# Late attention in strided-query order, with a new start for blocks 0 and 1: one change to a chunked-attention and gated feed-forward kernel

## The chip, the cores and the metric

The kernel runs on one core of a Trainium2 chip. The metric is device time in microseconds (us) of one execution. Each time below is a median of several executions; the profile shows one execution, and its span is about 2 us shorter than the time (260.4 and 262.46 us in the kernel before). The engines are named as the profile names them: PE (TensorE matmul), PEld (TensorE weight load), DVE (VectorE), ACT (ScalarE), POOL (GpSimd), SP (SyncE, here only the issuer of transfers).

## The reference

Chunked attention with a few memory rows, followed by a gated feed-forward network. Cut to what matters:

```python
# q, k, v: [4 batches, 8 heads, 768 rows, 64]; mem_k, mem_v: 8 rows per head
for c in range(24):                       # chunks of 32 queries
    l, r = max(0, 32*c - 16), min(768, 32*c + 40)
    k_full = concat(mem_k, k[:, :, l:r]); v_full = concat(mem_v, v[:, :, l:r])
    out[:, :, 32*c:32*c+32] = softmax(q_c @ k_full.T / 8) @ v_full
x = out as [3072 tokens, 512]
y = (relu(x @ w_gate) * (x @ w_val)) @ w_out       # 512 -> 1536 -> 512
```

The 3072 tokens are worked on as eight blocks of 384. A block has four attention steps of 96 queries; the keys of a step are a band of 120 rows and 8 memory rows. A block then has 12 feed-forward units (128 of the 1536 columns each: four gate matmuls, relu, four value matmuls, product) and three output products.

## The kernel before

Rows of q, k and v are loaded three to a partition, so that position 3i+t lies in partition i, slot t. After the transpose the queries are therefore in the order "t outer, i inner" (mod-3 order). The kernel before put them back into natural order when the exponential was written, which makes that write hop by three elements. These are the parts that matter (cuts marked):

```python
def diag(n):                              # block-diagonal queries, two DVE copies a block
    for x in range(2):
        dv(qd_t[n % 2][D * x:D * x + D, :, x, :], qT_t[n % 2][D * x:D * x + D].rearrange("p a t c -> p a (t c)"))
class Step:
    def scores(self):                     # ... early blocks 0, 1: two 64-row matmuls per head pair, from qp
        pe.matmul(o[...], lhsT=self.kb[:, a, j, :], rhs=qd_t[i][:, a]...)   # late: one 128-row matmul per pair
    def soft(self):                       # late:
        act.activation(e.rearrange("p h (c t) -> p h t c", t=R3),           # writes every third element
                       s_ps.rearrange("p h (t c) -> p h t c", t=R3), ACT.Exp, scale=SCALE)
    def mask(self):   dve.tensor_tensor(out=e, in0=e, in1=m8, op=ALU.mult)
    def values(self): ...                 # 8 matmuls with the masked exponentials as weights
    def norm(self):   ...                 # DVE: divide by the row sums
def dff(n, m):                            # one feed-forward unit
    ... gate matmuls; act Relu -> g_relu; value matmuls
    dve.tensor_tensor(out=gvT[n][:, m, c0:c1], in0=vl_ps, in1=g_relu[:, 0:w], op=ALU.mult)
# steady loop, block n beside the attention of block n+1
for u in range(NDC + NT):                 # 12 units, then 3 output products
    # u = 4, 6, 8, 10: scores and exp of step j, dff(u), mask; u = 6, 8, 10, 12: values and norm of step j
    ...
    if u == 0: diag(n + 1)
    if u == 1: bands(n + 1, pl)           # key bands, on POOL
```

In these traces ACT and DVE take their instructions in program order. So a long instruction there delays what stands behind it, whether that needs it or not: in the step shown below, the gate matmuls of a relu end at 125.00 us, but relu starts at 125.67, behind an exponential of 1.48 us that it does not read.

The softmax here doesn't subtract the row's maximum and nothing guards it: scores larger than these inputs give would overflow.

Of the kernel before, what the change touches and what calls it, by code (L numbers as in the profile page):

```python
# [15 lines left out]
def kernel(  # L16
# [49 lines left out]
    NG = [3]  # L66
# [18 lines left out]
    vx = wpool.tile([2 * NMEM, H, D], F32, name="vx")  # L85
    kx16 = wpool.tile([2 * NMEM, H, D], F16, name="kx16")
    vx16 = wpool.tile([2 * NMEM, H, D], F16, name="vx16")
    kT_t = [wpool.tile([128, R3 + 1, HP, 128], F16, name=f"kT{i}") for i in range(2)]
    qT_t = [wpool.tile([128, HP, R3, 128], F16, name=f"qT{i}") for i in range(2)]
    qd_t = [wpool.tile([128, HP, 2, MB], F16, name=f"qd{i}") for i in range(2)]  # L90
    kb_t = [wpool.tile([128, HP, NJ, 128], F16, name=f"kb{i}") for i in range(2)]
    vb_t = [wpool.tile([128, NJ, H, VW], F16, name=f"vb{i}") for i in range(2)]
    ex_t = [wpool.tile([128, H, 128], F16, name=f"ex{i}") for i in range(2)]
    id16 = wpool.tile([128, 128], F16, name="id16")
    step3 = wpool.tile([128, DW], F16, name="step3")
    selx = wpool.tile([2 * NMEM, 256], F16, name="selx")
# [12 lines left out]

    def build_mask(name, qb):  # L110
        m = wpool.tile([128, QB], F16, name=name)
        pool.memset(m, 1.0)
        for g in range(QB // 32):
            c = 3 * qb + g
            lo = max(32 * c - 16, 0) - starts[qb]
            hi = min(32 * c + 40, S) - starts[qb]
            sl = m[:, 32 * g:32 * g + 32]
            if lo > 0:
                pool.affine_select(out=sl, in_=sl, pattern=[[0, 32]], compare_op=ALU.is_ge,
                                   fill=0.0, base=-lo, channel_multiplier=1)  # L120
            if hi < BAND:
                pool.affine_select(out=sl, in_=sl, pattern=[[0, 32]], compare_op=ALU.is_ge,
                                   fill=0.0, base=hi - 1, channel_multiplier=-1)
        pool.affine_select(out=m, in_=m, pattern=[[0, QB]], compare_op=ALU.is_ge,
                           fill=1.0, base=BAND - 1, channel_multiplier=-1)
        return m

    masks = {}
# [57 lines left out]
    def diag(n):  # L186
        for x in range(2):
            dv(qd_t[n % 2][D * x:D * x + D, :, x, :], qT_t[n % 2][D * x:D * x + D].rearrange("p a t c -> p a (t c)"))  # L188

    def bands(n, eng, part=(0, 1)):  # L190
        i = n % 2
        kT, kb = kT_t[i], kb_t[i]

        def src(t, off, dims):
            return bass.AP(tensor=t.tensor, offset=t.offset + off, ap=[t.ap[0], [128, HP]] + dims)
# [6 lines left out]
        if 0 in part:  # L202
# [4 lines left out]
            else:  # L207
                e = kT_t[0]
                eng(dst(0, 16, [[R3, 35], [1, R3]]), src(kT, 0, [[1, 35], [TS, R3]]))
                eng(dst(0, 0, [[1, 1]]), src(e, 2 * TS + 122, [[1, 1]]))  # L210
                eng(dst(0, 1, [[R3, 5], [1, R3]]), src(e, 123, [[1, 5], [TS, R3]]))
                eng(dst(3, 0, [[R3, 40], [1, R3]]), src(kT, 88, [[1, 40], [TS, R3]]))
        if 1 in part:
            if i == 0:
                eng(dst(3, 112, [[1, NMEM]]), src(kT, R3 * TS, [[1, NMEM]]))
            eng(dst(0, BAND, [[128, NJ], [1, NMEM]]), src(kT_t[0], R3 * TS + NMEM, [[0, NJ], [1, NMEM]]))
# [5 lines left out]
    class Step:  # L222
        def __init__(self, n, j):
            self.n, self.j, self.kb, self.vb = n, j, kb_t[n % 2], vb_t[n % 2]
            self.early = n in EARLY
            self.mk = masks[kind(NJ * (n % 2) + j)]

        def scores(self):
            i, j = self.n % 2, self.j
            for a in range(HP):  # L230
                if self.early:
                    for x in range(2):
                        pe.matmul(PS[:, x, QB * a:QB * a + QB], lhsT=self.kb[D * x:D * x + D, a, j, :],
                                  rhs=qp[D * x:D * x + D, i, a, QB * j:QB * j + QB], start=True, stop=True)
                else:
                    o = PS[:, a // 2, 256 * (a % 2):256 * (a % 2) + 256].rearrange("p (x c) -> p x c", x=2)
                    pe.matmul(o[:, :, 0:QB].rearrange("p x (t c) -> p x t c", t=R3), lhsT=self.kb[:, a, j, :],  # L237
                              rhs=qd_t[i][:, a].rearrange("p x (t c) -> p x t c", t=R3)[:, :, :, PP * j:PP * j + PP],
                              start=True, stop=True)

        def soft(self):
            self.ex = ex_t[n_exp[0] % len(ex_t)]
            n_exp[0] += 1
            e = self.ex[:, :, 0:QB]
            if self.early:
                act.activation(e.rearrange("p (h b) c -> p b h c", b=2),  # L246
                               PS[:, 0:2, 0:384].rearrange("p b (h c) -> p b h c", h=4), ACT.Exp, scale=SCALE)
            else:
                s_ps = PS[:, 0:2].rearrange("p b (h c) -> p (b h) c", h=4)[:, :, 0:QB]
                act.activation(e.rearrange("p h (c t) -> p h t c", t=R3),  # L250
                               s_ps.rearrange("p h (t c) -> p h t c", t=R3), ACT.Exp, scale=SCALE)

        def mask(self):
            e = self.ex[:, :, 0:QB]
            m = self.mk
# [30 lines left out]
    def dff(n, m, c0=0, c1=MB):  # L286
# [13 lines left out]
        dve.tensor_tensor(out=gvT[n][:, m, c0:c1], in0=vl_ps, in1=g_relu[:, 0:w], op=ALU.mult)  # L300
# [5 lines left out]
    def outp(n, t, last=False):  # L306
# [5 lines left out]
        r0 = n * MB + 128 * t  # L312
        if last:
            act.copy(o_sb[:, 0:256], PS[:, o, 0:256])
            dv(o_sb[:, 256:512], PS[:, o, 256:512])
            sp.dma_start(out[r0:r0 + 128, 0:256], o_sb[:, 0:256])
            act.dma_start(out[r0:r0 + 128, 256:512], o_sb[:, 256:512])
        else:
            act.copy(o_sb, PS[:, o])  # L319
            sp.dma_start(out[r0:r0 + 128, :], o_sb)  # L320
# [3 lines left out]
    def turn3(c, n, a0):  # L324
        o = PS[:, bank(), 0:R3 * 128].bitcast(F16).rearrange("p (a t i) -> p a t i", a=2, t=R3)
        for a in range(2):
            for t in range(R3):
                w = kn[:, n % 2, t, a0 + a, :] if c == "k" else qn[:, n % 2, a0 + a, t, :]
                pe.transpose(o[:, a, t], w, id16)
        return o  # L330

    def turn_k3(n, a0):
        dv(kT_t[n % 2][:, 0:R3, a0:a0 + 2].rearrange("p t a c -> p a t c"), turn3("k", n, a0))

    def turn_q3(n, a0):
        act.copy(qp[:, n % 2, a0:a0 + 2].rearrange("p a (i t) -> p a i t", t=R3),
                 turn3("q", n, a0).rearrange("p a t i -> p a i t"))
# [4 lines left out]
    def gather_v(n, j, eng=None):  # L342
# [3 lines left out]
        sel = selx[:, 128:256] if (i, j) == (0, NJ - 1) else selx[:, 0:128]  # L346
        pe.matmul(o, lhsT=sel, rhs=vx16, start=True, stop=True)
        mm = [(s0 - MB * i - t, i, t) for t in range(R3)]
        if i == 1 and j == 0:
            mm += [(s0 - t, 0, t) for t in range(R3)]  # L350
        for e, (c, w, t) in enumerate(mm):
            pe.matmul(o[0:BAND], lhsT=step3[:, c:c + BAND], rhs=v16[:, w, :, t, :], start=False,  # L352
                      stop=(e == len(mm) - 1), skip_group_check=True)
        (eng or act.copy)(vb_t[i][:, j, :, 0:D], o)
# [3 lines left out]
    for c in "kq":  # L358
        load3(sp, c, 0, 0, 4)
        load3(sp, c, 0, 4, 4)  # L360
    load_kx(sp, 0)
    load3(sp, "v", 0, 0, 4)
    load3(sp, "v", 0, 4, 4)
    sp.dma_start(vx[NMEM:2 * NMEM], mem_v[0].rearrange("h n d -> n h d"))
    sp.dma_start(vx[0:NMEM], rows(v, 0, MB, NMEM))
    load3(sp, "k", 1)
    load3(sp, "q", 1)
    load3(sp, "v", 1)

# [4 lines left out]
    def keep(n):  # L374
        for _ in range(n):
            pe.matmul(PS[:, 7], lhsT=zero[:, 0:128], rhs=zero, start=True, stop=True)  # L376
# [6 lines left out]
    dve.memset(kT_t[0][:, R3, 0, 0:2], 0.0)  # L383
    act.activation(warm, warm, ACT.Exp)
    steps(id16, 0, -1)
    steps(step3, -DPAD, -R3)
    for c in (0, 128):
        steps(selx[:, c:c + 128], -(BAND - NMEM), -1)
    pool.memset(selx[0:NMEM, 0:128], 0.0)
# [4 lines left out]
    for m, qb in (("first", 0), ("int", 1)):  # L394
        masks[m] = build_mask(f"mask_{m}", qb)
# [16 lines left out]
    keep(9)  # L412
    cast3(dv, "k", 0, 0, 2)
    turn_k3(0, 0)
    cast3(dv, "k", 0, 2, 2)
    keep(2)
    turn_k3(0, 2)
    bands(0, dv, (0,))
    cast3(pl, "q", 0, 0, 2)
    act.copy(kx16, kx[:, 0])  # L420
    keep(1)
    turn_q3(0, 0)
    cast3(pl, "q", 0, 2, 2)
    keep(2)
    turn_q3(0, 2)
    o = PS[:, 3, 0:HP * NMEM].bitcast(F16).rearrange("p (a c) -> p a c", a=HP)
    for a in range(HP):
        pe.transpose(o[:, a], kx16[:, 2 * a:2 * a + 2, :].rearrange("n x d -> n (x d)"), id16[0:2 * NMEM, 0:2 * NMEM])
    act.copy(kT_t[0][:, R3, :, 0:2 * NMEM], o)
    bands(0, dv, (1,))  # L430
    keep(3)
    cast_v3(act.copy, 0, 0, 4)
    pl(vx16, vx)
    cast_v3(dv, 0, 4, 4)

    masks["last"] = build_mask("mask_last", NQB - 1)
    st = [Step(0, j) for j in range(NJ)] + [Step(1, j) for j in range(NJ)]

    def pipe(s, mid=(), end=()):
        if s < 2 * NJ:  # L440
            st[s].scores()
            st[s].soft()
            st[s].mask()
        for f in mid:
            f()
        if s < 2 * NJ:
            gather_v(s // NJ, s % NJ)
        if 1 <= s <= 2 * NJ:
            st[s - 1].values()
            st[s - 1].norm()  # L450
        for f in end:
            f()
        if s >= 2:
            st[s - 2].turn_pe(act.copy if s % 2 else dv)

    pipe(0, [lambda: keep(3)])
# [4 lines left out]
    pipe(1)  # L461
    cast3(pl, "q", 1, 0, 2)
    cast3(pl, "q", 1, 2, 2)
    pipe(2, (), [lambda: turn_k3(1, 0)])
    load_w(256, 256)
    pipe(3, (), [lambda: turn_k3(1, 2), lambda: turn_q3(1, 0)])
    cast_v3(pl, 1, 0, 4)
    cast_v3(pl, 1, 4, 4)
    turn_q3(1, 2)
    bands(1, dv)  # L470
    load_w(512, 512)
    load_w(1024, 512)
    for c in (0, 4, 8):
        load_wo(c)
    pipe(4)
    NG[0] = 4
    pipe(5)
    pipe(6, (), [lambda: dff(0, 0)])
    pipe(7, (), [lambda: dff(0, 1)])
    pipe(8, (), [lambda: dff(0, 2)])  # L480
# [149 lines left out]
```

## Time and profile before

| | before |
|---|---|
| time, median of 3 | 262.46 us |
| profiled span | 260.4 us |
| start: until block 1's first unit | 40.25 us |
| middle: from there until block 2's first unit | 47.75 us |
| five blocks with attention beside them (2 to 6) | 144.64 us |
| last block and end | 27.7 us |

The stages are read from the timeline: each boundary is the start of the first gate matmul of that unit. From the page, the busy time of the engines and the granted clock in the 40 slices of the span (tenths of full speed):

```profile
PE 235.4 (90%) x1611; PEld 131.5 (50%) x1611; DVE 124.1 (48%) x257; ACT 128.4 (49%) x197; POOL 49.3 (19%) x96
...
PEclk9998899999999899999999999999999999999999
```

PE is the bound, but 90% busy hides waits, since the records of matmuls overlap: most of those with 384 columns last 326 ns, and the next one starts after 162. A better measure is the distance between starts: 162 ns for 384 columns and 216 ns for 512 when nothing is in the way.

The groups of instructions by form (line, engine, operation, shapes, count, then busy us and mean ns, then the idle time ahead and who ended it):

```profile
L250 ACT ACTIVATE ex<-PS 128x768 f16<-128x768 f32 x24 | 35.2, 1468 | 20.3 <-PE PS L237 20.2
L246 ACT ACTIVATE ex<-PS 128x768 f16<-128x768 f32 x8 | 6.5, 814 | 3.8 <-PE PS L233 3.8
L188 DVE COPY qd<-qT 64x1536 f16<-64x1536 f16 x12 | 8.4, 696 | 4.8 <-DMA qT<-qn 4.8
```

The first two lines do the same arithmetic on the same 768 elements. L250 (late blocks) writes every third element, L246 (blocks 0 and 1) writes runs of 96: 1468 ns against 814.

One step of a steady block in the timeline (start, duration, engine, what, and in brackets the idle time ahead of it; other lines of the stretch are left out):

```profile
123.86 0.49 PE L237 MATMUL PS<-qd,kb 128*128 128x192 f16 x4
124.39 1.48 ACT L250 ACTIVATE ex<-PS 128x768 f16<-128x768 f32 x1 [1.42 <-PE PS L237]
125.67 0.51 ACT L296 ACTIVATE g_relu<-PS 128x384 f16<-128x384 f32 x1
126.14 0.81 PE L298 MATMUL PS<-xT,w_val_sb 128*128 128x384 f16 x4
126.22 0.56 DVE L300 TENSOR_TENSOR gvT<-PS,g_relu 128x384 f16<-128x384 f32 x1 [0.93 <-ACT g_relu L296]
126.69 0.55 DVE L257 TENSOR_TENSOR ex<-ex,mask_first 128x768 f16<-128x768 f16 x1
127.39 0.42 PE L261 MATMUL PS<-vb,ex 128*128 128x66 f16 x8 [0.43 <-DVE ex L257]
```

The exponential ends at 125.87. Relu stands behind it on ACT (its record starts at 125.67, since neighbours on one engine overlap a little in the record), then come the product gv, the mask, and the value matmuls. From the start of the matmul ahead of the values (the last of the four L298, near 126.63) to the values' start the trace has 0.75 us instead of 0.16, so PE loses about 0.59 us, in each of four steps of five blocks.

### The profile page before, as it was taken

The page shows a single profiled execution, that of the slowest core. Times are in us where ns is not written, and L with a number is a line of the kernel's source. Part 1 is how long each engine was busy: PE and PEld are TensorE (multiplying, and loading weights), DVE is VectorE, ACT ScalarE, POOL GpSimd, SP SyncE. Part 2 cuts the span into 40 slices and gives each one's busy share as a digit, 9 for nine tenths or more (in the row PEclk, how much of TensorE's full clock was granted, in tenths as well). Part 3 has the DMA queues.
Part 4 walks back from the last instruction along what each step waited for, and adds up shares of the span by engine and source line. Part 5 has one row for each costly group of instructions (what it writes and reads, how often), then busy time and mean ns, then how long its engine had stood idle before and what let it go on. Part 6 is the DMA issues. An engine that isn't in the chain of part 4 may idle for free.

```text
span 260.4 us, 4350 instructions
## 1 busy us (share of the span) xinstructions
PE 235.4 (90%) x1611; PEld 131.5 (50%) x1611; DVE 124.1 (48%) x257; ACT 128.4 (49%) x197; POOL 49.3 (19%) x96
## 2 busy tenths in 40 slices
PE   8895899999989698898989989898899998999993
PEld 3353565666444355544554555445564555446641
DVE  3776573444654057604673076605753276504410
ACT  2564554365357256643673457443772555333321
POOL 6499920000000500006000420006000500000000
PEclk9998899999999899999999999999999999999999
DMA  6999999849973997159941997179912801121012
GB/s 209 312 270 138 183 207 247 219 94 177 294 193 115 202 285 131 30 124 259 237 96 32 241 281 146 33 168 276 234 39 71 198 0 33 30 86 39 0 40 82
DMA packets 84381, 39.37 MB, mean 151 GB/s; under 512 B 57096, under 2 KB 81416, under 8 KB 84360
## 3 DMA queue, kind: packets, MB, share of 16 engines
q1 hardware_dynamic: 78408, 34.25, 54.2%
q0 software_dynamic: 5808, 4.72, 12.1%
q8 instruction: 12, 0.20, 0.3%
q10 hardware_dynamic: 144, 0.13, 0.1%
q14 instruction: 9, 0.07, 0.1%
HBM read 30.05 MB, written 6.29 MB: 140 GB/s over the span
## 4 chain that ended last, share of the span: by engine, by line
PE 56%; DVE 16%; issue 8%; DMA 7%; ACT 6%; SPq 3%; POOL 0%; ACTq 0%; DVEq 0%; POOLq 0%
PE PS L309 19%; PE PS L298 14%; PE PS L293 13%; DVE gvT L300 5%; DVE ex L257 5%; PE PS L261 4%; ACT g_relu L296 4%; DMA qT<-qn 3%; DVE x_big L270 3%; DMA vraw<-in_mem_v_dram 2%; PE PS L352 2%; DMA vx<-in_v_dram 2%; PE PS L237 2%; SPq L141 2%; DVE qd L188 1%
## 5 line engine op out<-in xcount | busy, mean ns | idle before, releaser
L300 DVE TENSOR_TENSOR gvT<-PS,g_relu 128x384 f16<-128x384 f32 x96 | 53.0, 556 | 96.3 <-PE PS L298 75.0
L293 PE MATMUL PS<-xT,w_gate_sb 128*128 128x384 f16 x384 | 78.7, 328 | 2.7 <-issue 2.2
L298 PE MATMUL PS<-xT,w_val_sb 128*128 128x384 f16 x384 | 79.1, 329 | 2.1 <-DVE gvT L300 1.9
L296 ACT ACTIVATE g_relu<-PS 128x384 f16<-128x384 f32 x96 | 47.8, 498 | 43.4 <-PE PS L293 22.4
L309 PE MATMUL PS<-w_out_sb,gvT 128*128 128x512 f16 x288 | 64.1, 379 | 0.0
L298 PEld LDWEIGHTS <-w_val_sb 128*128 128x128 f16 x384 | 37.8, 99 | 28.1 <-issue 3.8
L293 PEld LDWEIGHTS <-w_gate_sb 128*128 128x128 f16 x384 | 37.2, 98 | 25.9 <-issue 4.3
L250 ACT ACTIVATE ex<-PS 128x768 f16<-128x768 f32 x24 | 35.2, 1468 | 20.3 <-PE PS L237 20.2
L309 PEld LDWEIGHTS <-gvT 128*128 128x128 f16 x288 | 27.7, 98 | 31.4
L319 ACT COPY o_sb<-PS 128x512 f32<-128x512 f32 x23 | 13.5, 587 | 44.9 <-PE PS L309 43.0
L204 POOL COPY kb<-kT 128x320 f16<-128x320 f16 (+1 forms) x15 | 11.0, 830 | 130.2 <-DMA kT<-kn 130.2
L261 PE MATMUL PS<-vb,ex 128*128 128x66 f16 x256 | 13.6, 195 | 9.9 <-DVE ex L257 8.7
L270 DVE TENSOR_TENSOR x_big<-PS,rinv 96x512 f16<-96x512 f32 x32 | 22.0, 686 | 1.1
L261 PEld LDWEIGHTS <-ex 128*128 128x128 f16 x256 | 11.1, 99 | 20.4 <-ACT g_relu L296 15.6
L257 DVE TENSOR_TENSOR ex<-ex,mask_int 128x768 f16<-128x768 f16 x24 | 14.1, 586 | 7.3 <-ACT ex L246 3.9
L237 PE MATMUL PS<-qd,kb 128*128 128x192 f16 x96 | 11.8, 245 | 0.1
L188 DVE COPY qd<-qT 64x1536 f16<-64x1536 f16 x12 | 8.4, 696 | 4.8 <-DMA qT<-qn 4.8
L165 ACT CAST qn<-qraw 128x768 f16<-128x768 f32 x12 | 10.0, 836 | 0.0
L267 DVE RECIPROCAL rinv<-PS 96x8 f32<-96x8 f32 x32 | 6.4, 201 | 7.5 <-PE PS L261 5.4
L165 ACT CAST kn<-kraw 128x768 f16<-128x768 f32 x12 | 9.9, 827 | 0.0
L376 PE MATMUL PS<-zero 128*128 128x512 f16 x20 | 7.7, 519 | 1.3 <-DVE zero L378 1.3
L352 PE MATMUL PS<-v,step 128*120 128x512 f16 x27 | 8.8, 450 | 0.0
(90 smaller groups left out, 122.7 us busy)
## 6 DMA issues: line engine op xcount, KB each, us to landing
out_dram<-o_sb SPq DMA_DIRECT2D x23, 256.0 KB
vraw<-in_v_dram SPq DMA_DIRECT2D x24, 240.0 KB
kraw<-in_k_dram SPq DMA_DIRECT2D x7, 768.0 KB
qraw<-in_q_dram SPq DMA_DIRECT2D x7, 768.0 KB
w_out_sb<-in_moe_w_out_dram POOLq DMA_DIRECT2D x3, 512.0 KB, 18.1
w_gate_sb<-in_moe_w_gate_dram POOLq DMA_DIRECT2D x2, 512.0 KB, 10.4
w_val_sb<-in_moe_w_val_dram POOLq DMA_DIRECT2D x2, 512.0 KB, 12.0
kraw<-in_k_dram SPq DMA_DIRECT2D x2, 384.0 KB
```

Source lines behind the costliest of these rows:

```text
L165: eng(d.rearrange("p a t (x d) -> p a x t d", x=2), raw[c][:, i, 2 * a0:2 * a0 + 2 * na].rearrange("p (a x) t d -> p a x t d", x=2))
L237: pe.matmul(o[:, :, 0:QB].rearrange("p x (t c) -> p x t c", t=R3), lhsT=self.kb[:, a, j, :], rhs=qd_t[i][:, a].rearrange("p x (t c) -> p x ...
L250: act.activation(e.rearrange("p h (c t) -> p h t c", t=R3), s_ps.rearrange("p h (t c) -> p h t c", t=R3), ACT.Exp, scale=SCALE)
L257: dve.tensor_tensor(out=e, in0=e, in1=m8, op=ALU.mult)
L261: pe.matmul(PS[:, 2 + h // 4, VW * (h % 4):VW * (h % 4) + VW], lhsT=self.ex[:, h, :], rhs=self.vb[:, self.j, h, :], start=True, stop=True)
L270: dve.tensor_tensor(out=self.x.rearrange("p (b h d) -> p b h d", b=2, h=4), in0=o[:, :, :, 0:D], in1=rb, op=ALU.mult)
L293: pe.matmul(g_ps, lhsT=w_gate_sb[:, f, 128 * m:128 * m + 128], rhs=xTs[n][:, f, c0:c1], start=(f == 0), stop=(f == NFC - 1))
L296: act.activation(g_relu[:, 0:w], g_ps, ACT.Relu)
L298: pe.matmul(vl_ps, lhsT=w_val_sb[:, f, 128 * m:128 * m + 128], rhs=xTs[n][:, f, c0:c1], start=(f == 0), stop=(f == NFC - 1))
L300: dve.tensor_tensor(out=gvT[n][:, m, c0:c1], in0=vl_ps, in1=g_relu[:, 0:w], op=ALU.mult)
L309: pe.matmul(PS[:, o], lhsT=gvT[n][:, m, 128 * t:128 * t + 128], rhs=w_out_sb[:, m, :], start=(m == 0), stop=(m == NDC - 1))
L352: pe.matmul(o[0:BAND], lhsT=step3[:, c:c + BAND], rhs=v16[:, w, :, t, :], start=False, stop=(e == len(mm) - 1), skip_group_check=True)
```

## The change

It has several parts.

1. The late exponential writes contiguous rows. Queries stay in mod-3 order through mask, values, norm and x; the product gv, which DVE makes anyway, puts them in the order of three output tiles, and an output tile's rows are stored with a stride of three.
2. No block-diagonal queries: scores are eight 64-row matmuls on the transposed queries, so `diag` goes.
3. Middle: the attention of block 2 lies among the last 20 feed-forward units of blocks 0 and 1 instead of among six output products; weights and loads are asked for in another order.
4. Start: block 0's keys are banded by matmuls with a step matrix, its masks are added by a matmul with -30000, the memory values come by small transfers instead of matmuls, and there are four exponential buffers and two sets of score banks.

The core of the diff, cut:

```diff
-                    pe.matmul(o[:, :, 0:QB]..., lhsT=self.kb[:, a, j, :], rhs=qd_t[i][:, a]..., start=True, stop=True)
+                        pe.matmul(o.rearrange("p (t c) -> p t c", t=R3), lhsT=self.kb[r, a, j, :],
+                                  rhs=qT_t[i][r, a, :, PP * j:PP * j + PP], start=True, stop=True)
-                act.activation(e.rearrange("p h (c t) -> p h t c", t=R3),
-                               s_ps.rearrange("p h (t c) -> p h t c", t=R3), ACT.Exp, scale=SCALE)
+            act.activation(self.ex[:, :, 0:QB].rearrange("p (h b) c -> p b h c", b=2),
+                           PS[:, self.sb:self.sb + 2, 0:HP * QB].rearrange("p b (h c) -> p b h c", h=HP), ACT.Exp, scale=SCALE)
+            dve.tensor_tensor(out=gvT[n][:, m].rearrange("p (t j c) -> p t j c", t=R3, j=NJ),
+                              in0=vl_ps.rearrange("p (j t c) -> p t j c", t=R3, j=NJ),
+                              in1=g_relu.rearrange("p (j t c) -> p t j c", t=R3, j=NJ), op=ALU.mult)
+            dst = bass.AP(tensor=out.tensor, offset=out[n * MB + t, 0].offset, ap=[[R3 * DM, 128], [1, DM]])
... the start (block 0)
+    def keys(a, eng): ...            # 8 matmuls per head pair: kn x step3, kx x selx -> kb_t[0][:, a]
+            if self.n == 0: pe.matmul(PS[...], lhsT=id16, rhs=m4, ...)      # mask of -30000
+    for j in range(NJ):
+        sp.dma_start(vb_t[0][BAND:128, j, :, 0:D], vm16)                    # memory values, also for vb_t[1]
... between blocks 0 and 1 (program order)
+    G_(3); key_ends(ac); bands(1, dv, (0,)); bands(1, pl, (1,)); P_(2); T_(1); P_(3)
+    cast3(pl, "q", 1, 0, 2); cast3(dv, "q", 1, 2, 2); load_w(256, 256); turn_q3(1, 0, ac); T_(2); T_(3)
+    turn_q3(1, 2, ac); ...; load_w(512, 512); S_(4)
... the middle
-    pl(raw["k"][0:1, 0, 0, 0, 0:1], w_val_sb[0:1, 0, DFF - 1:DFF])          # load block 2 after all of w_val
+    pl(raw["k"][0:1, 0, 0, 0, 0:1], w_gate_sb[0:1, 0, 1023:1024])           # ... after w_gate up to column 1023
     load_kq(2)
+    load_w(1024, 512)
+    cast_kx(pl, 1)
+    pl(gate, w_val_sb[0:1, 0, DFF - 1:DFF])
+    load_wo(0)
+    hook = {0: [cast k], 1: [cast k, turn_k(2)], 2: [cast q], 3: [cast q, turn_q(2)], 4: [load_v(2, 0..3)],
+            5: [bands(2, pl)], 6: [gate on v, load_wo(4), load_wo(8)], 10, 11: [cast_v], 12, 13: [loads of block 3]}
+    su, vu = (11, 13, 15, 17), (13, 15, 17, 19)                             # scores / values of block 2 by unit
```

Here S_ is scores, exp and (block 1) mask; G_ gathers the values of a step by matmul; P_ is value matmuls and norm; T_ transposes x; `turn_k`/`turn_q` are transposing transfers issued by SP.

## The prediction

> **What bounds it now.** TensorE: 90% of a 260.4 us span on the page. In the timeline 384-column matmuls repeat every 162 ns, 512-column ones every 216; at that pace all matmuls need 217 us. Some 43 us are PE waits, half clock and start-up, placed by the timeline:
>
> - Steady blocks (starts 88.0, 117.7, 146.7, 175.2, 204.1, 232.65: about 28.8 us each, against 23.4 us for the last, which has no attention beside it). In each, PE stops four times for 0.59 us before the value matmuls, which wait for the mask multiply. The chain: scores, exp 1.47 us (L250), relu 0.5, gv 0.56, mask 0.55, values; the long exp holds back relu, gv and mask. Once per block gv also waits behind the two block-diagonal query copies (L188, 0.70 us each): 0.3 to 1.0 us of PE.
> - 66.1 to 88.0: only six output products (2.6 us each) hide block 2's attention; PE waits 0.9 us for the cast of v, 0.4 for a mask, 2.2 for the transposed x, then runs at half clock until 92 (320 ns per matmul), 1.7 us more.
> - 0 to 40.25: 14 us over the pace: a chain of copies for block 0's keys, scores at 11.0, 2.2 us idle until 23.5 behind block 1's key bands, and half clock. [...]
>
> **What the change does.**
> 1. Late exp writes contiguous rows. The same 768 elements written so in blocks 0 and 1 take 0.81 us (L246), so 0.65 us is the scattered write. Relu comes 0.5 us earlier; gv is then limited by its own matmuls, and the stall falls from 0.59 to about 0.1: 5 x 4 x 0.5 = 10 us. The reordering moves to gv on DVE, in runs of 32; like the norm (0.69 us for 512 in runs of 64) I expect it to stay at 0.56 to 0.6 us.
> 2. No diagonal copies: 8.4 us of DVE, 2.7 us of PE waits in blocks 3 to 7. Scores become eight 64-row matmuls in pairs that start 3 ns apart (L233), but entering and leaving that mode costs about 0.1 us each in the trace[...]. Net +0.04 us a step, 1 us in all.
> 3. Block 2's attention spreads over 20 feed-forward units: 47.75 us (40.25 to 88.0) become about 44.5, and the half clock after it goes.
> 4. Blocks 0 and 1: keys banded on PE (+2.6 us) instead of three 0.65 us copies and more; masks by matmul (+0.3 us PE a step, -0.57 DVE); eight 0.3 us matmuls for memory values go to DMA. I estimate block 1's first unit at 35.5 instead of 40.25.
>
> **Sum.** 35.5 + 44.5 + 5 x 26.4 + 27.75 (unchanged last block) = 239.8, plus 2 us between span and time, plus 1 us for what I overlook: **243 us**, 8 in 10 between **238** and **250**. Faster by over 2%: **0.95**; within 2%: **0.04**; slower: **0.01**.
>
> **Right if** late exp shows about 0.81 us, values hardly wait for the mask, blocks start every 26 to 26.5 us, and no half clock follows block 2's start.
>
> **Wrong if** gv gets slower through its permuted rows (each 0.1 us comes straight back as a stall), the later weight and k/q loads arrive late (DMA is saturated until 45 us), or block 2's casts at the first units hold back relu.

35.5 + 44.5 + 132 + 27.75 came to 239.8, and with 2 and 1 us to 242.8, given as 243. What the trace of the kernel before shows of the half clock in the start is a granted clock of 0.50 from 23.98 to 27.39 us, in which 512-column matmuls repeat every 427 ns instead of 216. The +2.6 and +0.3 us of PE in point 4 are estimates; 5920 and 768 columns at the traced 216 ns for 512 would give 2.5 and 0.3.

## The result, and the profile after

249.01 us median of four executions, against 262.23 us median of the kernel before (four executions; the 262.46 above is the median of three of them). The ratio is 0.9482, 95% interval 0.9412 to 0.9551: faster. A ratio is the mean time of one kernel's fast runs over that of the other's of the same rounds, so it is not quite the ratio of the medians. The time lies inside the predicted range. The gain is 13.2 us, where 19.5 were forecast (262.46 - 243).

One of the four executions took 479.14 us, the other three 248.85 to 249.07. The profile fell in that slow one. There, 512-column matmuls repeat every 443 ns, some every 558, from the first to the last. That is a third pace, neither the 216 ns of full clock nor the 427 ns that the first matmuls of the kernel before (1.7 to 4.7 us) and its half-clock stretch show. What clock was granted cannot be read: this trace holds no clock record at all (its page has no PEclk row), and the clock of 1.00 that is printed for it is only what stands there when there is none. These are two groups of that slow execution's page:

```profile
L311 PE MATMUL PS<-xT,w_val_sb 128*128 128x384 f16 x384 | 155.2, 565 | 0.0
L316 DVE TENSOR_TENSOR gvT<-PS,g_relu 128x384 f16<-128x384 f32 x72 | 40.2, 558 | 258.1 <-PE PS L311 258.1
```

The matmul's mean is 565 ns, against 329 in the kernel before; DVE's product has its usual 558. Only PE was slow. None of the 52 further executions, of the changed kernel and of all the builds below, showed this. So it is set aside as an execution in which PE stayed slow throughout, its cause is open, and all readings below are from a fast execution of the same kernel, the run a0_again (247.4 us span).

From the page of the changed kernel's fast profile, the two lines that answer to those of before:

```profile
PE 235.4 (95%) x1740; PEld 130.2 (53%) x1740; DVE 113.7 (46%) x237; ACT 115.1 (47%) x197; POOL 46.7 (19%) x101
...
PEclk9999599999999999999999999999999999999999
```

PE has the same busy time in a shorter span; DVE and ACT lost 10 and 13 us. The single 5 in the clock row, at 25 to 31 us, becomes important below. The groups that answer to those of before:

```profile
L263 ACT ACTIVATE ex<-PS 128x768 f16<-128x768 f32 x32 | 25.7, 811 | 15.5 <-PE PS L257 11.5 <-PE PS L254 3.1
L316 DVE TENSOR_TENSOR gvT<-PS,g_relu 128x384 f16<-128x384 f32 x72 | 40.1, 557 | 88.5 <-PE PS L311 87.2 <-ACT g_relu L309 0.9
L314 DVE TENSOR_TENSOR gvT<-PS,g_relu 128x384 f16<-128x384 f32 x24 | 13.4, 557 | 16.0 <-PE PS L311 16.0
```

The exponential takes 811 ns everywhere. The product with permuted rows (L316, late blocks) takes 557 ns, exactly as the one without (L314, blocks 0 and 1): the reordering cost nothing there. The copies L188 are gone.

The same step of the same block in the timeline (again without the other lines):

```profile
119.58 0.34 PE L257 MATMUL PS<-qT,kb 64*128 64x96 f16 x8
119.96 0.81 ACT L263 ACTIVATE ex<-PS 128x768 f16<-128x768 f32 x1 [0.44 <-PE PS L257]
120.71 0.49 ACT L309 ACTIVATE g_relu<-PS 128x384 f16<-128x384 f32 x1
121.43 0.56 DVE L316 TENSOR_TENSOR gvT<-PS,g_relu 128x384 f16<-128x384 f32 x1 [0.53 <-PE PS L311]
121.81 0.81 PE L311 MATMUL PS<-xT,w_val_sb 128*128 128x384 f16 x4
121.91 0.55 DVE L270 TENSOR_TENSOR ex<-ex,mask_first 128x768 f16<-128x768 f16 x1
122.60 0.41 PE L274 MATMUL PS<-vb,ex 128*128 128x66 f16 x8
```

Now gv waits for its own value matmuls (L311), no longer for relu, and the values hardly wait: start to start is 0.30 us there instead of 0.75 (0.16 would be no wait).

By stage, in us of the profiled execution:

| stage | before | predicted | after | predicted gain | gain |
|---|---|---|---|---|---|
| start | 40.25 | 35.5 | 42.34 | 4.75 | -2.09 |
| middle | 47.75 | 44.5 | 45.48 | 3.25 | 2.27 |
| five blocks | 144.64 | 132.0 | 132.31 | 12.64 | 12.33 |
| last block, end | 27.7 | 27.75 | 27.3 | 0 | 0.4 |

The five blocks came out as forecast, 26.46 us each. The start, whose gain of 4.75 us was forecast, lost 2.1 us. That is most of the difference, and most of the experiments are about it.

What the start looks like in the changed kernel, by stretches (columns: stretch, its length, busy us and counts of PE, PEld, DVE, ACT, POOL, then the granted clock, the busy share of the transfer engines, GB/s):

```profile
20.00:25.00 5.00, 2.49 (x47) 1.87 (x46) 3.66 (x13) 1.90 (x4) 4.11 (x7) 1.00 1.03 135
25.00:30.00 5.00, 4.28 (x32) 2.58 (x32) 2.35 (x5) 2.56 (x4) 2.89 (x6) 0.50 1.29 194
30.00:35.00 5.00, 4.94 (x40) 2.48 (x38) 1.75 (x4) 3.13 (x6) 1.69 (x3) 0.82 1.12 256
```

PE is half idle from 20 to 25 (busy for 2.49 of the 5.00 us, and for 1.16 of the 3.40 us from 21.6 to 25.0), then runs at half clock. The idleness is in short pieces: no listed wait of PE in this trace is longer than the 1.53 us below. From the clock column the half clock lasts 5.0 x 0.50 x 2 + 5.0 x 0.18 x 2 = 6.8 us; the kernel before has 0.58 over the 4 us from 24 to 28, so 3.4 us. This is how the changed kernel usually runs: six of its seven fast executions have a mean granted clock of 0.984 to 0.986, the profiled one 0.985. And in the timeline:

```profile
21.13 0.84 POOL L177 CAST qn<-qraw 128x768 f16<-128x768 f32 x1
...
21.79 0.20 DVE L219 COPY kb<-ke 128x4 f16<-128x4 f16 x1 [1.03 <-ACT ke L369]
...
23.28 0.41 PE L274 MATMUL PS<-vb,ex 128*128 128x66 f16 x8 [1.53 <-DVE x_big L283]
...
24.58 0.83 DVE L177 CAST qn<-qraw 128x768 f16<-128x768 f32 x1
...
27.18 0.66 PE L254 MATMUL PS<-qp,kb 64*128 64x96 f16 x12 [0.61 <-ACT qp L383]
```

DVE stands 1.03 us for the key ends, with the norm of step 2 behind it; PE therefore waits 1.53 us with the values of step 3; the second half of block 1's q is cast only at 24.58, and block 1's scores begin at 26.2 and go on at 27.18. In the kernel before they begin at 23.50.

The first scores, of block 0, come at 11.75 instead of 10.99. Its key bands are complete earlier (9.82 instead of 10.93, the end of the last copy into kb), but q is later: the cast of its second half starts at 9.38 instead of 8.09, after a short wait for the transfer in both.

### The profile page after: what moved, and what is told of

Read it like the earlier page. It is cut to its first block, busy times and chain, and to the rows that moved or that the text cites. A ratio compares the mean times of both kernels' runs of the same rounds, so it can differ in the third digit from the quotient of the medians.

```text
span 477.4 us, 4618 instructions
## 1 busy us (share of the span) xinstructions
PE 468.0 (98%) x1740; PEld 196.2 (41%) x1740; DVE 114.0 (24%) x237; ACT 116.9 (24%) x197; POOL 46.8 (10%) x101
## 4 chain that ended last, share of the span: by engine, by line
PE 97%; DVE 1%; ACT 0%; issue 0%
PE PS L306 28%; PE PS L327 28%; PE PS L311 28%; PE PS L274 3%; PE PS L398 3%; PE PS L257 2%; PE PS L417 2%; PE PS L361 1%; PE PS L247 1%; PE PS L254 1%; DVE x_big L283 1%; PE PS L382 0%; PE PS L292 0%; ACT qp L383 0%; PE PS L375 0%
## 5 line engine op out<-in xcount | busy, mean ns | idle before, releaser
L311 PE MATMUL PS<-xT,w_val_sb 128*128 128x384 f16 x384 | 155.2, 565 | 0.0
L306 PE MATMUL PS<-xT,w_gate_sb 128*128 128x384 f16 x384 | 151.6, 556 | 0.0
L327 PE MATMUL PS<-w_out_sb,gvT 128*128 128x512 f16 x288 | 136.0, 680 | 0.0
L316 DVE TENSOR_TENSOR gvT<-PS,g_relu 128x384 f16<-128x384 f32 x72 | 40.2, 558 | 258.1 <-PE PS L311 258.1
L311 PEld LDWEIGHTS <-w_val_sb 128*128 128x128 f16 x384 | 57.1, 149 | 77.2 <-issue 77.2
L306 PEld LDWEIGHTS <-w_gate_sb 128*128 128x128 f16 x384 | 52.8, 143 | 68.5 <-issue 66.5
L327 PEld LDWEIGHTS <-gvT 128*128 128x128 f16 x288 | 42.4, 149 | 87.1 <-issue 87.1
L213 POOL COPY kb<-kT 128x480 f16<-128x480 f16 (+1 forms) x18 | 13.6, 854 | 254.4 <-DMA kT<-kn 195.4
L263 ACT ACTIVATE ex<-PS 128x768 f16<-128x768 f32 x32 | 25.8, 810 | 41.1 <-PE PS L257 33.2
L274 PEld LDWEIGHTS <-ex 128*128 128x128 f16 x264 | 21.4, 132 | 16.2 <-issue 15.0
L314 DVE TENSOR_TENSOR gvT<-PS,g_relu 128x384 f16<-128x384 f32 x24 | 13.4, 558 | 52.7 <-PE PS L311 52.7
L257 PE MATMUL PS<-qT,kb 64*128 64x96 f16 x192 | 10.0, 232 | 0.0
```

Of the source, the lines that this page charges most:

```text
L257: pe.matmul(o.rearrange("p (t c) -> p t c", t=R3), lhsT=self.kb[r, a, j, :], rhs=qT_t[i][r, a, :, PP * j:PP * j + PP], start=True, stop=True)
L263: act.activation(self.ex[:, :, 0:QB].rearrange("p (h b) c -> p b h c", b=2), PS[:, self.sb:self.sb + 2, 0:HP * QB].rearrange("p b (h c) -> ...
L274: pe.matmul(PS[:, 2 + h // 4, VW * (h % 4):VW * (h % 4) + VW], lhsT=self.ex[:, h, :], rhs=self.vb[:, self.j, h, :], start=True, stop=True)
L306: pe.matmul(g_ps, lhsT=w_gate_sb[:, f, 128 * m:128 * m + 128], rhs=xTs[n][:, f, c0:c1], start=(f == 0), stop=(f == NFC - 1))
L311: pe.matmul(vl_ps, lhsT=w_val_sb[:, f, 128 * m:128 * m + 128], rhs=xTs[n][:, f, c0:c1], start=(f == 0), stop=(f == NFC - 1))
L316: dve.tensor_tensor(out=gvT[n][:, m].rearrange("p (t j c) -> p t j c", t=R3, j=NJ), in0=vl_ps.rearrange("p (j t c) -> p t j c", t=R3, j=NJ ...
```

## The experiments

All are builds on one of the two kernels, correct, with fast profiles. An execution over 1.5% above the fastest of its kernel counts as slow; medians in the table are over all executions, ratios over fast ones. The stages of each in the profiled execution:

| run | median us | start | middle | five blocks | span |
|---|---|---|---|---|---|
| before | 262.46 | 40.25 | 47.75 | 144.64 | 260.4 |
| a0_again (changed kernel) | 249.92 | 42.34 | 45.48 | 132.31 | 247.4 |
| e1_exp_only | 250.81 | 40.63 | 47.16 | 134.58 | 250.1 |
| e2_exp_nodiag | 252.64 | 40.25 | 47.14 | 132.52 | 247.6 |
| f1_queue_order | 256.43 | 49.81 | 44.89 | 132.37 | 254.3 |
| f2_engine_order | 252.85 | 41.06 | 50.05 | 132.37 | 250.8 |
| f3_fill_gaps | 251.52 | 44.74 | 44.89 | 132.76 | 249.7 |
| f2b_engine_order_weights_early | 248.85 | 40.23 | 46.19 | 133.06 | 246.8 |
| f3b_fill_gaps_free_bank | 250.81 | 40.38 | 48.94 | 132.68 | 249.3 |
| f23b_order_and_fill | 250.49 | 39.76 | 51.46 | 132.52 | 251.0 |
| e3_old_start_new_middle | 251.28 | 43.22 | 46.48 | 132.34 | 249.4 |
| g1_order_v_before_transposes | 247.94 | 40.13 | 44.90 | 132.74 | 245.0 |
| g2_order_fill_v_before_transposes | 248.32 | 39.80 | 44.88 | 132.67 | 244.6 |

A caution for reading it: even the fast executions of one kernel differ by up to 4 us (before: 260.1 to 263.9), and some medians contain slow ones: two of e2's four (254.3 and 254.7), one each of f3b's and g2's, and several of the kernel before. So differences of 1 or 2 us are read from the stages of the traces, not from the medians; but each trace is one execution. All builds lie below the kernel before with their whole intervals.

### a0_again: the changed kernel once more

> The changed kernel as it is, for a trace at full clock (the profiled execution on record ran its matmuls at half pace[...], from end to end). If that was a matter of one execution: about 249 us, 512-column matmuls at 216 ns, late exp 0.81 us, steady blocks about 26.4 us. If the changed kernel brings it on itself, this run shows about 479 us again in some executions.

249.92 us median, 248.94 to 251.01; ratio 0.9586 (0.9515 to 0.9657). 512-column matmuls repeat at 216 ns (443 to 558 in the slow execution), the late exponential takes 811 ns, blocks 26.46 us. The 479 us did not come back.

### e1_exp_only and e2_exp_nodiag: parts 1 and 2 alone on the kernel before

```diff
 e1: -                act.activation(e.rearrange("p h (c t) -> p h t c", t=R3), s_ps.rearrange(...), ACT.Exp, scale=SCALE)
     +                act.activation(e, s_ps, ACT.Exp, scale=SCALE)
     + masks in mod-3 order, gv with permuted rows, output rows with stride 3
 e2: e1, and -  diag(n), qd_t   + eight 64-row score matmuls from qT_t, bands(n + 1, pl) at u == 0
```

> The kernel before with part 1 alone: late exp writes contiguous rows, the queries keep their mod-3 order until the gating product, the block-diagonal copies stay. Theory (the 1.47 us exp is what makes the value matmuls wait 0.59 us, four times in each of five blocks): 10 us less, about 252 us. Rival (the wait comes from the diagonal copies or from in-order DVE work, the exp only hides in it): less than 3 us gained, 259 us or more.

> The run with part 1 alone, and in addition no block-diagonal queries: scores as eight 64-row matmuls from the transposed queries. Theory: the 2.7 us of waits behind the copies go, 1 us comes back[...]: about 250 us. Rival[...]: no faster than the run with part 1 alone, or slower.

e1: 250.81 us median, ratio 0.9609 (0.9547 to 0.967). The five blocks fall from 144.64 to 134.58, 10.06 us, where the prediction had 10. The rival (under 3 us) falls. The exponential of the late blocks reads the same scores, only the order of its write has changed, and it takes 811 ns instead of 1468:

```profile
L255 ACT ACTIVATE ex<-PS 128x768 f16<-128x768 f32 x24 | 19.5, 811 | 11.9 <-PE PS L242 9.5 <-DVE gvT L307 1.6
```

What is left in e1 are four waits of 0.3 to 1.1 us in the five blocks. In the two long ones (0.9 and 1.1) gv stands behind the diagonal copies; in the two short ones the values wait for the mask.

e2: the five blocks fall by another 2.06 us to 132.52 (predicted: 2.7 less 1.0). Not all of this is part 2. In block 2 the gain is 1.16 us, and there e1 still runs 3.4 us at half clock (from 89.1) and e2 does not. The other four blocks gain 0.90 us: they lose about 2.1 us of waits (e1's four against four times its block 6, 26.22 us, which has none), and pay about 0.24 us a block for the 64-row scores (26.46 against 26.22). The price of the 64-row matmuls is seen in the trace: about 95 ns extra on entering them (258 ns after a 384-column matmul instead of 162) and on leaving them (135 ns instead of 40), 24 times each. The times do not show the gain: fast executions took 249.33 and 250.94 us in e2, 249.85 to 251.82 in e1. The profiles do (250.1 and 247.6 us), but e1's is its longest execution and e2's its shortest.

So in the profiled executions e2, parts 1 and 2 alone, already has the changed kernel's span within 0.2 us (247.6 and 247.4). By stages, parts 3 and 4 together brought almost nothing there: the new start costs 2.1 us, the new middle gives 1.7 back (47.14 to 45.48), the end 0.4. Whether they make other executions shorter is not shown: e2 has only two fast ones (spans 247.6 and 249.2 us).

### f1_queue_order, f2_engine_order, f3_fill_gaps: why does the start lose?

```diff
 f1: vm load behind v; vm16 cast behind the first q casts; the eight copies vb<-vm behind the loads of q 1 and v 1
 f2: +    cast3(pl, "q", 1, 0, 2); cast3(pl, "q", 1, 2, 2)        # right after load_w(0, 256)
     +    G_(3); key_ends(ac); P_(2); bands(1, ...); turn_q3(1, 0, ac); T_(1); turn_q3(1, 2, ac); P_(3); T_(2); load_w(256, 256)
 f3: +    keepb(n): n matmuls of 248 zero columns into PS[:, 3, 264:512], at six places between T_(0) and S_(4)
```

Three theories are tested. Q: the added transfers in the queue hold back q. D: the order of work on DVE and POOL between blocks 0 and 1 makes block 1's scores late. H: the half clock eats the gain.

> The changed kernel; only the order of transfers differs: the small load of memory values goes behind the v loads, its cast behind the first query cast, and the eight small copies of memory values (7 us of the queue's issue time in the trace) behind the q and v loads of block 1, which are then issued about 4 us earlier. Theory Q (the early stage gained nothing because the added transfers hold back q): first scores about 1 us earlier than 11.7, block 1's scores 2 to 4 us earlier than 26.2, time 2 to 4 us less. Theory D (it is the order of work on VectorE and GpSimd between blocks 0 and 1): block 1's scores move by less than 1 us, time within 1 us of the changed kernel.

> The changed kernel; only the order of work between blocks 0 and 1 differs: GpSimd casts both halves of block 1's q directly after its k (before it waits for the key bands), and VectorE normalises step 2 before it copies the key bands, so it does not wait for the key ends. Theory D: block 1's scores at about 24.6 instead of 26.2 to 27.2, the first unit of block 1 at about 40 instead of 42.3, time about 2 us less. Theory Q: no change, as q lands too late either way. Theory H (the half clock from 24.9 to 31.7 is what eats the gain): less than 1 us as long as the half clock stays.

> The changed kernel with 41 idle-filling matmuls of 248 columns (on an unused part of a values bank) put where TensorE waits between 18.7 and 27.2 us. Theory H: the clock stays full, the stretch from 24.9 to 31.7 runs at 216 ns per 512 columns instead of 427, and the time falls by 2.5 to 3.5 us. Theory D or Q alone: TensorE was waiting for others anyway, so less than 1 us.

All three were slower than the changed kernel, each for a reason of its own.

f1: 256.43 us. The first scores gain only 0.2 us (11.56), and the copies of the memory values, moved back, are on the path. They take 8.45 us of the queue's issue time (3.06 and 4.13 us for four each in the changed kernel), and the first value matmuls wait for them:

```profile
12.69 8.45 SPq L466 DMA_DIRECT2D vb<-vm  x8
...
20.70 0.62 PE L274 MATMUL PS<-vb,ex 128*128 128x66 f16 x8 [4.63 <-DMA vb<-vm]
```

PE then runs at half clock for 17.1 us of the start (0.90, 0.50, 0.75, 0.68, 0.50 and 0.54 in the 4 us stretches from 16 to 40). As a test of theory Q it is a miss, since it put a new wait in the way; it shows that the eight 8 KB copies are dear (the 8.45 us) and that the changed kernel had put them where they just fit.

f2: block 1's scores start at 24.67, as theory D said (24.6), and block 1's first unit at 41.06; the half clock there lasts 3.4 us instead of 6.8. But the middle takes 50.05 us: PE waits 1.9 us at 47.4 for the cast of block 2's q, and 1.9 and 1.2 us at 60.1 and 65.6 for its v. The edit had also moved a weight load back, from 21.9 to 24.2 us, and block 2's k and q wait for such a landing.

f3: the half clock is halved but not gone (granted clock 0.66 from 25 to 30 us, so 3.4 us). The fillers wrote to a bank that holds values and waited for the norm, which made PE late:

```profile
24.26 0.48 PE L460 MATMUL PS<-zero 128*128 128x248 f16 x3 [2.74 <-DVE x_big L283]
```

Start 44.74. So f3 does not test theory H. But f1 and f3 show something by accident: with a late start the middle takes 44.89 us in both, with no wait above 0.2 us after block 1's first unit. That is what the middle costs when block 2's data is in time.

### f2b, f3b, f23b, e3: the same without the mishaps, and a fourth theory

Theory B: the transfers of the first 60 us limit what an earlier start can bring.

```diff
 f2b: f2, but load_w(256, 256) and load_w(512, 512) directly after POOL's q casts, and all of bands(1) on DVE
 f3b: f3 with keepb into PS[:, 7, 0:248] (a score bank, unused there)
 f23b: f2b with 31 fillers in banks 7 and 1
 e3:  e2's start, with the changed kernel's middle
```

> As the run with the other order of work between blocks 0 and 1, but GpSimd issues the weight loads for columns 256 to 1023 before it waits for anything of block 1 (about 21 to 23.5 us instead of 24.2 to 27.5 there), so that block 2's k and q, which wait for the landing of these weights, are asked for at about 28 us (34.5 there, 30.5 in the changed kernel). Theory D: block 1's scores at about 24.7, block 1's first unit at about 41 or earlier, and now no waits for block 2's k, q and v in the units after; time about 1.5 us under the changed kernel. Theory B (transfers of the first 60 us are the limit, an earlier TensorE only waits for them later): no faster than the changed kernel, with waits of over 1 us for block 2's k, q or v.

> The gap filling again, its matmuls now into a score bank that nobody uses between 16.5 and 27 us (in the first try they had to wait for the normalisation, since they wrote to a values bank, and made TensorE wait instead of filling its gaps). Theory H: no half clock between 24.9 and 31.7, block 1's first unit at about 39 to 40 instead of 42.3, time 2 to 3.5 us under the changed kernel. Theory B: block 1's first unit earlier as well, but the gain comes back as waits for block 2's k, q and v, so under 1 us in time.

> Both: the order with early weights, and 31 filling matmuls of 248 columns in free banks. Theories D and H added: block 1's scores at about 24.5, full clock, block 1's first unit at about 37.5 to 38.5, time about 4 us under the changed kernel, about 245. Theory B: block 1's first unit as early, but waits for block 2's data of 2 us or more, time within 1.5 us of the changed kernel.

> The kernel before with contiguous exp and no block-diagonal queries, and in addition the changed kernel's middle stage (block 2's attention among 20 feed-forward units, its weights and loads in the new order), with the old start. If the new start is what costs 2 us and the new middle gains 2 us: block 1's first unit at about 40.3, block 2's first unit 45.5 us later, time about 247, 2 us under both the changed kernel and the run without the new middle. Theory B: the k and q of block 2 come too late for the earlier units, waits of over 1 us there, time about 249.

Here are the stretches from 25 to 30 us of f2b and of f3b, with columns as above (0.50 in the changed kernel):

```profile
25.00:30.00 5.00, 4.82 (x33) 2.62 (x34) 2.24 (x5) 2.77 (x5) 2.65 (x5) 0.66 1.27 202
25.00:30.00 5.00, 4.98 (x52) 3.24 (x50) 2.79 (x6) 3.73 (x7) 3.27 (x6) 1.00 1.25 177
```

f2b: block 1's scores start at 24.93, 1.3 us earlier than in the changed kernel, and its first unit at 40.23, 2.1 us earlier. The first 1.3 us are theory D. The other 0.8 us come after that, where the half clock is shorter too (3.4 us instead of 6.8), so f2b alone does not separate D from H. f3b: no half clock in the start (PE is busy for 9.98 of the 10 us from 20 to 30, against 6.77 in the changed kernel), first unit at 40.38, 2.0 us earlier, though block 1's scores begin 0.8 us later (27.04). That is theory H by itself. Both at once, f23b: 39.76, so the two overlap and do not add up. Part of this is the fillers' own price: eight of them stand from 26.20 to 27.04 in f23b, and the gather of values behind them starts at 27.04; in f2b it starts at 26.14.

But little or nothing of the gain reaches block 2. The middle grows from 45.48 to 46.19, 48.94 and 51.46, and block 2's first unit comes at 86.42, 89.32 and 91.22, against 87.82 in the changed kernel. In f3b and f23b the waits are followed by another 3.4 us of half clock (from 61.5 and 58.6), which makes up about 1.7 us of the longer middle. What PE's suppliers wait for between 40 and 70 us, first in the changed kernel, then in f23b (waiter, data, us in total, times, longest):

```profile
POOL kb L213 <- DMA kT<-kn: 7.8, 1, 7.8
...
DVE vb L184 <- DMA vraw<-in_mem_v_dram: 1.0, 1, 1.0
```

```profile
POOL kb L213 <- DMA kT<-kn: 10.3, 1, 10.3
DVE vb L184 <- DMA vraw<-in_mem_v_dram: 7.3, 2, 5.5
```

The timeline of f23b shows why. Block 2's k is cast by 43.1, 2.6 us earlier than in the changed kernel, and its transposing transfer issued at once. Yet the key bands, which wait for it, start later:

```profile
43.19 2.44 SPq L191 DMA_TRANSPOSE kT<-kn  x1
43.44 0.75 POOL L451 DMA_DIRECT2D w_out_sb<-in_moe_w_out_dram  x1
...
45.75 4.74 SPq L196 DMA_TRANSPOSE qT<-qn  x1
50.58 0.54 SPq L169 DMA_DIRECT2D vraw<-in_v_dram  x1
...
54.53 2.67 POOL L213 COPY kb<-kT 128x480 f16<-128x480 f16 x3 [10.34 <-DMA kT<-kn]
```

From the issue to the bands it is 11.3 us, with a weight load issued 0.25 us after it; in the changed kernel 6.1 (45.76 to 51.85), with the same load issued 2.45 us ahead of it, at 43.31; in a steady block of the kernel before, with an odd block's three quarters of the data, 4.1 (142.78 to 146.85). For 0.5 MB of keys (128 x 2048 elements of f16) the 11.3 and 6.1 us give at least 46 and 86 GB/s, an estimate from these times. That the weight load is what slows the transfer is not shown. And block 2's v stands behind both transposes in the same queue, so it is asked for between 49.5 and 51.1 us in the changed kernel, f2b, f3b, f23b and e3 alike, however early the units come.

e3: the start was 43.22, not 40.3, although its order of work up to there is e2's (only later weight loads are gone). The reason is in the clock. From 24 to 36 us, e3 has 0.70, 0.50 and 0.52 in its three stretches of 4 us:

```profile
24.00:28.00 4.00, 3.63 (x35) 2.27 (x36) 1.61 (x4) 1.67 (x3) 1.04 (x4) 0.70 1.05 155
28.00:32.00 4.00, 3.85 (x26) 1.94 (x26) 1.54 (x4) 2.11 (x4) 1.66 (x3) 0.50 1.12 258
32.00:36.00 4.00, 4.00 (x19) 2.09 (x20) 1.45 (x3) 1.37 (x3) 0.60 (x1) 0.52 1.20 240
```

That is 10.2 us of half clock; e2 has 0.57, 1.00 and 1.00, so 3.4 us. PE was busy for 0.85 us between 20 and 24 in e3 and for 1.27 us in e2. This is not an accident of one execution: e3's four have a mean granted clock of 0.970 to 0.979, e2's two fast ones 0.990 and 0.986. So half clock came in one, two or three times 3.4 us at a time (e2 and the kernel before, the changed kernel, e3). That a little more or less idleness decides between them is my reading of it; no run varies that alone. The middle was 46.48 us, with waits for block 2's bands and v again. e3 is a miss as a better version.

### g1 and g2: v ahead of the transposes

```diff
      load_kq(2)
 +    for j in range(NJ): load_v(2, j)          # was at unit 4, behind turn_k(2) and turn_q(2)
      cast_kx(pl, 1)                            # now ahead of load_w(1024, 512)
 -    load_wo(0)                                # at about 43 us
 +    6: [load_wo(0), load_wo(4), load_wo(8)]   # after the key bands, about 54 us
```

g1 is f2b with this, g2 is f23b with this.

> As the run with the other order and early weights, and in addition: block 2's v is asked for right after its k and q (about 29 us) instead of behind the two transposing transfers (51 us there), the weights of columns 1024 on wait for block 2's k, and the first part of the output weights is asked for with the two others (about 50 us) instead of at 43 us, so that it does not run beside the transposing transfers. Theory B as a matter of order (v stuck behind transposing transfers[...]): key bands of block 2 start by 48 us instead of 51.3, no waits for v at 54 to 62 us, block 2's first unit at about 85, time about 247, 2 us under the changed kernel. Theory B as a matter of volume (the first 60 us of transfers are full anyway): the waits move to the feed-forward units that need columns 1024 on or to the first output product, and the time stays within 1 us of 249.

> The same transfer order together with the filling matmuls. Theory B as order: full clock from 21 us on, block 1's first unit at about 39.8, block 2's at about 84.5 to 85.5, time about 245. Theory B as volume: as before 249 to 250, waits elsewhere between 40 and 75 us.

The middle is 44.90 and 44.88 us, with no wait above 0.2 us in it: the 44.89 of f1 and f3 again, now behind an early start. In f23b it was 51.46. So it was the order of the transfers, not their volume: the same bytes are moved. The key bands start at 50.5 and 50.4, later than the 48 us expected, but soon enough. Block 2's first unit comes at 85.03 and 84.68 (87.82 in the changed kernel). Which of the moves counts (v earlier, the output-weight load away from the transposes, the weights of columns 1024 on behind `cast_kx`) was not tried apart.

The spans are 245.0 and 244.6 us, against 247.4. In time g1 has a median of 247.94 and a ratio of 0.9512 (0.9455 to 0.9568), g2 248.32 and 0.9523 (0.9461 to 0.9585). Both beat the kernel before. Against the changed kernel (ratios 0.9482 and 0.9586) the intervals overlap. So do the spans: both profiles are the shortest of six executions, and the fast ones run from 245.0 to 248.7 and from 244.6 to 247.1, the changed kernel's seven from 246.9 to 249.1. That g1 and g2 are faster than the changed kernel is therefore shown for the stages of the traces, and not for the times.

## Why the prediction was right or wrong, point by point

- **Range: right.** 249.01 us in 238 to 250, though near the upper end; the gain was 13.2 us where 19.5 were forecast. The range held because it was 12 us wide: one of its terms, the start, missed by 6.8 us.
- **"the stall falls from 0.59 to about 0.1: 5 x 4 x 0.5 = 10 us": right.** e1, that part alone, takes 10.06 us off the five blocks. The exponential fell from 1468 to 811 ns.
- **"I expect it to stay at 0.56 to 0.6 us" (gv with permuted rows): right.** 557 ns with and without. It got no slower, so the "each 0.1 us comes straight back as a stall" was the author's estimate and was not tried.
- **"2.7 us of PE waits" against "1 us in all" for the 64-row scores: right in kind, the sum partly by luck.** Net 1.7 predicted, 2.06 measured from e1 to e2, of which 1.16 in block 2 with a half clock that e2 escaped. The other four blocks gained 0.90; the price was about 1.2 us in five blocks.
- **"47.75 us become about 44.5": right in kind, 1 us short.** 45.48. The middle without waits takes 44.9 (f1, f3, g1, g2).
- **"and the half clock after it goes": right.** In the changed kernel PE no longer waits in the 20 us before block 2's first unit, where the kernel before waits 2.2 us. e2, with the old middle, has no half clock in block 2 either (26.46 us), but still that wait (2.5 us, as in e1, which has the half clock); so one trace without it proves little, and the wait that is gone proves more.
- **"I estimate block 1's first unit at 35.5 instead of 40.25": wrong, and this is the step that failed.** It came at 42.34, and this 6.8 us is nearly all of the missing gain. The prediction added up what leaves DVE and PE and did not follow the chain from block 0 to block 1. The runs show two things in it, about 2 us each and overlapping: the order on DVE and POOL (f2b, which also shortens the half clock), and the half clock that PE falls into after being half idle from 20 to 25 us (granted clock 0.50 from 25 to 30; 1.00 in f3b, where the idle time is filled). With both removed the start is still 39.8 us (f23b and g2), of which up to 0.9 us are the fillers themselves; the cause of the rest of the way to 35.5 stays open.
- **"the later weight and k/q loads arrive late": the worry was in place, but for a start that did not come.** The "saturated" is seen in the kernel before: the busy share of the transfer engines is 1.10 to 1.25 in each 5 us stretch from 5 to 45 us. In the changed kernel block 2's data is just in time for units that start at 42.3. As soon as the start is made earlier, the old order of transfers takes the gain back (f2, f3b, f23b), through the transposed keys and v. An estimate of 35.5 would have needed another transfer order as well.

## What to carry to other kernels

The strided write by ACT (1468 ns instead of 811) was paid by everything behind it in program order (without it, in e1, the five blocks took 10.06 us less): let the exponential write contiguous rows and give the reordering to an instruction that does not mind it, here a DVE product from PSUM whose duration did not change (557 ns with and without). An estimate for a start-up stage must follow the chain of waits and the transfer queue; a sum of the work removed is no estimate, and an earlier PE gained little or nothing here as long as the loads of the next block stood behind slow transposing transfers in one queue (f23b: block 1's first unit 2.6 us earlier, 11.3 us from the issue of k's transfer to the bands, block 2's first unit 3.4 us later). Look at PE's clock after every stretch of half idleness: nearly the same start took 40.25 us in e2 and 43.22 in e3, with 3.4 and 10.2 us of half clock.
